# Storing x2 and its logits batch by batch: 64-row transfers in place of two-batch transfers in a delta-attention and two-MoE kernel

## The chip, the cores and the metric

The kernel runs on one core of a Trainium2 chip, as one program. The metric is device time in microseconds (us) of one execution. Before the change the median of three runs is 911.99 us (910.92 to 912.21).

## What is computed

Three stages follow one another (B = 4 batches, 8 heads, S = 768 positions, head size 48; 3072 tokens of 384 features):

```python
for t in range(S):                                    # attention: a delta rule per head
    y[:, :, t] = einsum('bhd,bhde->bhe', q_t, state)
    v_old = einsum('bhde,bhd->bhe', state, k_t)
    state += b_t * outer(k_t, v_t - v_old)
x = y.transpose(0, 2, 1, 3).reshape(B * S, 384)       # tokens: batch-major
h = x @ w_in; x2 = (h * sigmoid(h)) @ w_out           # first MoE: 384 -> 2048 -> 384
logits = x2 @ w_gate; e = argmax(logits)              # second MoE: eight experts, top 1
out = x2, and for tokens with x2 @ w_skip > 0:
out += softmax(logits)[e] * (relu(x2 @ w1[e]) @ w2[e])
```

Products are made in float32 accuracy by splitting each operand into a high and a low part (`gh`/`gl`, `exh`/`exl`, `ew`), so one product takes three matmul groups.

## The kernel before

**Stages.** The sequence is cut into 12 chunks of 64 positions (`NCH`, `CH`). In `period(c)` attention of chunk c runs beside the first MoE of chunk c-1 (`l1`, `l2`: sixteen blocks of 128 hidden features) and the finish of chunk c-2. One chunk holds 4 x 64 = 256 tokens, as columns of the tile `x`. After the last chunk `moe(NCH - 1)` and `finish(NCH - 1, ...)` run with no attention beside them; then comes the expert stage: for each of the eight experts, gather its tokens, transpose them, two products, and a scatter of the results into `out`.

**Finish of a chunk.** `x2out` (lines 718 to 739) takes the 256 columns in two halves `hf`. A half holds the 64 positions of batch 2*hf and the 64 positions of batch 2*hf + 1. TensorE transposes it and multiplies by the gate and skip weights at once (`xr`); ScalarE copies the 384 features and VectorE sums the ten logit columns into the tile `xs`, 128 partitions x 394 floats: partitions 0 to 63 are one batch, 64 to 127 the other. Two transfers then leave from SyncE: `x2s<-xs`, all 394 columns, into a table in DRAM from which the experts gather, and `out_dram<-xs`, the 384 features, into the result. `route1` and `route2` find each token's expert and its place, and `scatter` writes token numbers into the lists `lst` by an indirect transfer from GpSimd.

**After the last chunk.** `index_last` (line 772) computes the experts' token numbers `idx_t` on TensorE and VectorE, without going through `lst` for the last chunk. `warm(30)` issues 30 small matmuls. GpSimd then issues six indirect gathers `xg<-x2s,idx_t` (`gather_e`, line 894, experts 0 to 2, two halves each). A gather reads any row of `x2s`, so it can start only when every store into `x2s` has landed. `tr_e` transposes the gathered rows (`etp`), `el1` and `el2` are the two products (`ehp`, `yp`), `eout` writes the results.

**Weights of the experts.** `load_e` loads one expert's weights in eight pieces of 384 KB (`eraw`, eight buffers), ScalarE and then VectorE or GpSimd split a piece (`ew`), which frees its buffer for the next expert. For expert 1 GpSimd's splits are placed behind the gathers.

**What sets the order.** Every engine and every queue works in order. From chunk 2 on, the class `InOrder` keeps instructions as the Python code issues them; its helper at line 43 records every operation, so nearly all rows of the profile read L43 and are told apart by tile names. The rest is ordered by a scheduler; in the last two finishes it puts `out_dram<-xs` of half 0 ahead, since that needs ScalarE's copy alone. All plain transfers leave by SyncE's one queue (SPq), in order. They name a view of DRAM:

```python
ov = out.rearrange("(b s) f -> b s f", b=B)[2 * hf:2 * hf + 2, c * CH:(c + 1) * CH, :]
sv = x2s.rearrange("(b s) f -> b s f", b=B)[2 * hf:2 * hf + 2, c * CH:(c + 1) * CH, :]
nc.sync.dma_start(out=sv, in_=xs)
nc.sync.dma_start(out=ov, in_=xs[:, 0:DM])
```

Of the kernel before, what the change touches and what calls it, by code (L numbers as in the profile page):

```python
# [57 lines left out]
def kernel(  # L58
# [25 lines left out]
    nc = InOrder(tc)  # L84
    NCH, B, _, _, NP, CH = qk.shape
    D = ki.shape[-1]
    H, S = 2 * NP, NCH * CH
    NTOK, DM = out.shape
# [32 lines left out]
    x2s = dram.tile([NTOK, WX], F32, name="x2s")  # L121
# [591 lines left out]
    def x2a(c):  # L713
        xt = x2_t[c, "t"] = rot.tile([128, KD, B * CH], F32, tag="k3", name="xt")
        nc.vector.tensor_copy(out=xt[:, 0:2], in_=mm[c][0])
        act_copy(out=xt[:, 2], in_=mm[c][1][:, 0])

    def x2out(c):

        if (c, "t") not in x2_t:  # L720
            x2a(c)
        xt = x2_t.pop((c, "t"))
        for hf in range(2):
            ts = slice(hf * 128, (hf + 1) * 128)
            xp = ps_1.tile([128, KD, 128 + NL], F32, tag="l1", name="xr")
            for jj in range(KD):
                nc.tensor.matmul(xp[:, jj], lhsT=xt[:, jj, ts], rhs=iwg[:, jj], start=True, stop=True)
            xs = rot.tile([128, WX], F32, tag="k15", name="xs", bufs=2)
            seen["x2"] = nc.scalar.activation(
                out=xs[:, 0:DM].rearrange("p (j f) -> p j f", j=KD), in_=xp[:, :, 0:128], func=AF.Copy  # L730
            )
            nc.vector.tensor_reduce(
                out=xs[:, DM:WX], in_=xp[:, :, 128:].rearrange("p j e -> p e j"), axis=AX.X, op=ALU.add
            )
            ov = out.rearrange("(b s) f -> b s f", b=B)[2 * hf:2 * hf + 2, c * CH:(c + 1) * CH, :]
            sv = x2s.rearrange("(b s) f -> b s f", b=B)[2 * hf:2 * hf + 2, c * CH:(c + 1) * CH, :]
            nc.sync.dma_start(out=sv, in_=xs)
            nc.sync.dma_start(out=ov, in_=xs[:, 0:DM])
            x2_t[c, hf] = xs

    def route1(c):
# [384 lines left out]
    def finish(c, part):  # L1126
        if part == 0:
            x2out(c)
        elif part == 1:
            route1(c)  # L1130
        else:
            route2(c)
# [200 lines left out]
    for j in range(2):  # L1333
        nc.sync.dma_start(
            out=idx_h[:, j],
            in_=lst[j].rearrange("(e r) c -> e (r c)", e=NE)[:, 0:CAP].rearrange("e (p a) -> p e a", a=2),
# [6 lines left out]
    for part in range(3):  # L1343
# [7 lines left out]
        out=cnt_i, in0=ct, scalar1=float(127 - CAP), scalar2=None, op0=ALU.add  # L1351
# [111 lines left out]
```

## Time and profile before

| | |
|---|---|
| median of three runs | 911.99 us |
| the profiled execution, its own time | 911.39 us |
| its span (first to last instruction) | 909.6 us |
| TensorE matmul (PE) busy | 816.8 us, 90% of the span |
| TensorE weight load (PEld) busy | 780.5 us, 86% |
| VectorE (DVE) busy | 619.0 us, 68% |
| ScalarE (ACT) busy | 473.6 us, 52% |
| GpSimd (POOL) busy | 367.9 us, 40% |
| stores `x2s<-xs` | 24, of 197.0 KB |
| stores `out_dram<-xs` | 24, of 192.0 KB |

The busy shares are means over stages with different limits; PE and PEld overlap. KB are units of 1024 bytes. [...] A duration of an SPq row is the time that the queue's sequencer took to issue the transfer, not the time of the transfer.

### The profile page before, as it was taken

The numbers are of one execution on the slowest core, as the hardware profiler recorded it, in microseconds if no ns is written. First come the engines' busy times: TensorE is split into PE (matmuls) and PEld (weight loads), VectorE is DVE, ScalarE is ACT, GpSimd is POOL, SyncE is SP. The second block draws the span as 40 slices with busy tenths as digits, with TensorE's granted clock in tenths as the row PEclk, the third lists the DMA queues.
The fourth block names the chain that finished last, engine by engine and source line by source line (L and its number), as shares of the span: only waits on it lengthen the run. The fifth ranks groups of instructions, "written<-read, shape, count | busy, mean of one in ns | idle before, by whom it ended". The sixth has DMA issues, their size and how long they took to land. (4 is left out here: it accounts for less than half of the span.)

```text
span 909.6 us, 25993 instructions
## 1 busy us (share of the span) xinstructions
PE 816.8 (90%) x10385; PEld 780.5 (86%) x10385; DVE 619.0 (68%) x1776; ACT 473.6 (52%) x1290; POOL 367.9 (40%) x533
## 2 busy tenths in 40 slices
PE   8175978798899999999999999999999939999994
PEld 8174977797899999999999999999998938999994
DVE  4998895797777978777786877779223018765731
ACT  3257974336464655647465665745454334555520
POOL 5477663141333334333333333334336333454320
PEclk6565898898999999999999999999999968999998
DMA  8963211122230414132140414120036116766300
GB/s 296 399 212 108 77 31 34 55 58 64 80 125 18 127 53 139 51 104 90 31 145 27 132 51 139 53 65 19 29 111 204 19 51 192 257 208 218 112 21 24
DMA packets 64914, 96.09 MB, mean 106 GB/s; under 512 B 9290, under 2 KB 46232, under 8 KB 64784
## 3 DMA queue, kind: packets, MB, share of 16 engines
q1 hardware_dynamic: 61968, 89.69, 31.0%
q0 software_dynamic: 2816, 4.65, 1.7%
q8 instruction: 83, 1.36, 0.6%
q14 instruction: 47, 0.39, 0.2%
HBM read 80.79 MB, written 12.91 MB: 103 GB/s over the span
## 5 line engine op out<-in xcount | busy, mean ns | idle before, releaser
L43 POOL TENSOR_TENSOR gl<-gf,gh 128x256 fp32r<-128x256 f32 x192 | 149.7, 780 | 347.9 <-ACT gf L43 305.9
L43 PE MATMUL hp<-x,w 128*128 128x256 f32 x1728 | 256.5, 294 | 7.2 <-DMA x<-x 2.7
L43 PEld LDWEIGHTS hp<-x,w 128*128 128x128 f32 x1728 | 224.6, 194 | 15.3 <-DVE xs L43 4.4
L43 PE MATMUL xp<-gh,w 128*128 128x256 f32 x1152 | 172.1, 285 | 6.7 <-ACT gh L43 6.3
L43 PEld LDWEIGHTS xp<-gh,w 128*128 128x128 f32 x1152 | 153.6, 192 | 7.9 <-ACT gh L43 6.9
L43 DVE SCALAR_TENSOR_TENSOR tmp<-X,nw,Gi 128x126 f32<-128x126 f32 (+22 forms) x341 | 137.2, 402 | 10.4
L43 ACT ACTIVATE gh<-hp 128x256 fp32r<-128x256 f32 x192 | 73.3, 382 | 136.1 <-PE hp L43 135.2
L43 DVE TENSOR_TENSOR X<-X,tmp 128x126 f32<-128x126 f32 (+22 forms) x341 | 102.6, 301 | 8.6
L43 PE MATMUL xp<-gl,w 128*128 128x256 f32 x576 | 103.9, 288 | 2.1 <-POOL gl L43 2.0
L43 PEld LDWEIGHTS xp<-gl,w 128*128 128x128 f32 x576 | 83.2, 192 | 3.9 <-POOL gl L43 3.0
L43 ACT ACTIVATE gf<-hp 128x256 f32<-128x256 f32 x192 | 72.7, 379 | 4.7 <-POOL gl L43 4.6
L43 PE MATMUL ehp<-exh,ew 128*128 128x256 f32 x384 | 66.9, 284 | 0.0
L43 ACT ACTIVATE SU<-St 32x192 f32<-32x192 f32 (+1 forms) x176 | 63.6, 361 | 2.7
L43 ACT ACTIVATE ew<-eraw 128x768 fp32r<-128x768 f32 x64 | 53.3, 843 | 21.0 <-PE yp L43 15.4
L43 PE MATMUL g<-kq,KtB 128*128 128x128 f32 (+1 forms) x384 | 55.5, 303 | 8.9 <-DVE PQ L43 5.6
L43 DVE COPY_PREDICATED PQ<-mU,g 128x512 f32<-128x512 uint8 x44 | 32.2, 738 | 45.3 <-ACT G L43 39.1
L43 DVE TENSOR_TENSOR ew<-eraw,ew 128x768 fp32r<-128x768 f32 x48 | 49.9, 1046 | 18.0 <-ACT ew L43 12.0
L43 PEld LDWEIGHTS g<-kq,KtB 128*128 128x128 f32 x384 | 52.1, 216 | 10.1 <-DVE PQ L43 6.2
L43 DVE TENSOR_TENSOR vp<-vp,ru 64x192 f32<-64x192 f32 x92 | 31.5, 345 | 41.7 <-PE ru L43 38.5
L43 PEld LDWEIGHTS ehp<-exh,ew 128*128 128x128 f32 x384 | 58.8, 191 | 0.0
L43 PE MATMUL yp<-ew,egh 128*128 128x384 f32 x256 | 57.6, 342 | 0.3 <-ACT egh L43 0.3
L43 POOL TENSOR_TENSOR ew<-eraw,ew 128x768 fp32r<-128x768 f32 x16 | 30.2, 1892 | 57.0 <-ACT ew L43 56.7
(144 smaller groups left out, 1283.6 us busy)
## 6 DMA issues: line engine op xcount, KB each, us to landing
eraw<-in_w_dram SPq DMA_DIRECT2D x64, 384.0 KB
kq<-in_qk_dram SPq DMA_DIRECT2D x44, 256.0 KB
PQ<-in_qp_dram SPq DMA_DIRECT2D x44, 256.0 KB
ki<-in_ki_dram SPq DMA_DIRECT2D x44, 192.0 KB
raw<-in_w_out_dram SPq DMA_DIRECT2D x16, 384.0 KB
raw<-in_w_in_dram SPq DMA_DIRECT2D x16, 384.0 KB
x2s<-xs SPq DMA_DIRECT2D x24, 197.0 KB
v<-in_v_dram SPq DMA_DIRECT2D x24, 192.0 KB
```

Source lines behind the costliest of these rows:

```text
L43: r = f(*args, **kw)
```

## The change

Each of the two stores of a half becomes two stores, one per batch: 64 partitions of `xs` into 64 consecutive rows of `x2s`, or of `out`. The same bytes go to the same places.

```diff
-            ov = out.rearrange("(b s) f -> b s f", b=B)[2 * hf:2 * hf + 2, c * CH:(c + 1) * CH, :]
-            sv = x2s.rearrange("(b s) f -> b s f", b=B)[2 * hf:2 * hf + 2, c * CH:(c + 1) * CH, :]
-            nc.sync.dma_start(out=sv, in_=xs)
-            nc.sync.dma_start(out=ov, in_=xs[:, 0:DM])
+            for i in range(2):
+                t0 = (2 * hf + i) * S + c * CH
+                nc.sync.dma_start(out=x2s[t0:t0 + CH, :], in_=xs[i * CH:(i + 1) * CH])
+            for i in range(2):
+                t0 = (2 * hf + i) * S + c * CH
+                nc.sync.dma_start(out=out[t0:t0 + CH, :], in_=xs[i * CH:(i + 1) * CH, 0:DM])
```

On SyncE's queue, the finish of an early chunk (here the first one in the program), as a piece of the difference; the shapes are those of the DRAM side:

```order
 L43 DMA x<-x 16x3x512 x2
-L43 DMA x2s<-xs 2x64x394
-L43 DMA out_dram<-xs 2x64x384
-L43 DMA x2s<-xs 2x64x394
-L43 DMA out_dram<-xs 2x64x384
+L43 DMA x2s<-xs 64x394 x2
+L43 DMA out_dram<-xs 64x384 x2
+L43 DMA x2s<-xs 64x394 x2
+L43 DMA out_dram<-xs 64x384 x2
 L43 DMA kq<-in_qk_dram 128x512 x2
 L43 DMA v<-in_v_dram 128x384
```

Four issues became eight; what stands ahead and behind is the same.

On SyncE's queue, the finish of the last chunk, before:

```order
L43 DMA idx_h<-lst_86 128x8x2
L43 DMA out_dram<-xs 2x64x384
L43 DMA x2s<-xs 2x64x394 x2
L43 DMA out_dram<-xs 2x64x384
L43 DMA eraw<-in_w_dram 128x3x256
```

and with the change:

```order
L43 DMA idx_h<-lst_86 128x8x2
L43 DMA out_dram<-xs 64x384
L43 DMA x2s<-xs 64x394 x2
L43 DMA out_dram<-xs 64x384
L43 DMA x2s<-xs 64x394 x2
L43 DMA out_dram<-xs 64x384 x2
L43 DMA eraw<-in_w_dram 128x3x256
```

The last `x2s` store was third of the four and is now sixth of the eight: ahead of it stand four 64-row stores of half 0 and one of its own half. Apart from SyncE's queue, the instructions of all engines stand in the same order as before.

## Rows read from the trace of the kernel before

**Rows 1.** Busy time by stretch (us, engines' busy us and counts, PEclk, DMA share, GB/s)

```profile
250.00:300.00 50.00, 49.75 (x770) 47.50 (x769) 38.60 (x120) 29.51 (x89) 18.98 (x31) 1.00 0.25 79
727.00:750.00 23.00, 7.95 (x57) 6.94 (x56) 5.00 (x29) 8.71 (x13) 7.35 (x9) 0.67 0.15 48
800.00:850.00 50.00, 49.19 (x352) 48.67 (x350) 32.41 (x65) 28.25 (x54) 21.79 (x16) 1.00 0.67 205
```

**Rows 2.** Waits, 715 to 790 us (us in total, times, longest)

```profile
PE etp L43 <- DMA xg<-x2s,idx_t: 12.0, 3, 11.3
POOL xg L43 <- DMA x2s<-xs: 10.3, 1, 10.3
```

**Rows 3.** Timeline around the gathers (start, us, instruction, idle before and releaser)

```profile
729.31 0.52 SPq L43 DMA_DIRECT2D out_dram<-xs  x1
...
729.95 2.94 SPq L43 DMA_DIRECT2D x2s<-xs  x2
...
730.02 0.19 DVE L43 TENSOR_REDUCE xs<-xr 128x10 f32<-128x30 f32 x1
...
734.52 3.36 PE L43 MATMUL g<-one 128*128 128x128 bf16 x30
734.56 0.97 POOL L43 DMA_INDIRECT lst<-ids,si  x1 [0.30 <-issue]
734.71 0.17 DVE L43 TENSOR_TENSOR idx_t<-idx_f,px 128x16 int32<-128x16 f32 x1 [0.46 <-PE px L43]
745.84 1.04 POOL L43 DMA_INDIRECT xg<-x2s,idx_t  x1 [10.31 <-DMA x2s<-xs]
...
749.23 0.87 PE L43 MATMUL etp<-iwg,xg 128*128 128x128 f32 x3 [11.35 <-DMA xg<-x2s,idx_t]
...
753.42 3.64 POOL L43 TENSOR_TENSOR ew<-eraw,ew 128x768 fp32r<-128x768 f32 x2
...
764.96 0.85 ACT L43 ACTIVATE ew<-eraw 128x768 fp32r<-128x768 f32 x1 [2.30 <-DMA eraw<-in_w_dram]
...
766.13 0.97 PE L43 MATMUL yp<-ew,egh 128*128 128x384 f32 x4 [0.29 <-ACT egh L43]
```

**Rows 4.** Busy time by stretch: loads at the start, and around the gathers

```profile
20.00:40.00 20.00, 5.72 (x27) 5.53 (x26) 18.73 (x66) 5.59 (x16) 5.92 (x11) 0.50 1.04 400
...
738.00:741.00 3.00, 0.00 (x0) 0.00 (x0) 0.00 (x0) 0.00 (x0) 0.00 (x0) 0.94 0.14 45
...
752.00:755.50 3.50, 3.50 (x19) 3.50 (x18) 3.31 (x7) 0.88 (x2) 3.18 (x4) 0.51 0.38 103
755.50:760.00 4.50, 4.37 (x31) 4.05 (x31) 4.50 (x8) 1.25 (x4) 1.56 (x1) 1.00 0.39 99
```

**Rows 5.** DMA in the stretch 735 to 745 us

```profile
DMA packets 365, 0.46 MB, mean 46 GB/s; under 512 B 70, under 2 KB 365, under 8 KB 365
```

**Rows 6.** Timeline of one period: SyncE's queue, and ScalarE's first use of `kq`

```profile
234.24 0.56 SPq L43 DMA_DIRECT2D x2s<-xs  x1
...
235.53 3.10 SPq L43 DMA_DIRECT2D x2s<-xs  x1
238.68 3.41 SPq L43 DMA_DIRECT2D out_dram<-xs  x1
242.14 4.30 SPq L43 DMA_DIRECT2D kq<-in_qk_dram  x2
...
255.99 0.84 ACT L43 ACTIVATE KtB<-kq 64x256 f32<-64x256 f32 x2
```

**Rows 7.** Timeline: two pairs of transfers and the instruction that waits for them

```profile
143.87 1.21 SPq L43 DMA_DIRECT2D x<-x  x2
...
147.43 0.83 PE L43 MATMUL hp<-x,w 128*128 128x256 f32 x5 [0.71 <-DMA x<-x]
...
707.74 2.71 SPq L43 DMA_DIRECT2D idx_h<-lst  x2
...
714.56 0.17 DVE L43 TENSOR_TENSOR idx_f<-idx_h 128x16 f32<-128x16 int32 x1 [13.99 <-DMA idx_h<-lst]
```

## The prediction

> **What bounds the kernel now.** I looked first at busy time by stretch, since a mean over stages tells nothing here [rows 1]. In a period of the attention TensorE is busy 49.75 of 50 us, and in the expert stage 49.19 of 50. There a faster transfer can buy next to nothing. Between the two, from 727 to 750 us, it is busy 7.95 of 23 us. That hole is where stores could matter, so the waits of that stretch came next [rows 2]: GpSimd's first gather waits 10.3 us for `x2s<-xs`, and TensorE waits 11.3 us for what the gather brings. The timeline gives the chain [rows 3]. SyncE issues `out_dram<-xs` of half 0 at 729.31 and the two `x2s<-xs` from 729.95 on. The token numbers `idx_t` are ready at 734.71 + 0.17 = 734.88, GpSimd is through with its last scatter at 734.56 + 0.97 = 735.53, and then both stand still until 745.84. TensorE's transposes follow at 749.23.
>
> Why do three stores, some 600 kB (192 + 197 + 197 KB of 1024 bytes), need 729.31 to 745.84, which is 16.5 us? In the middle of that time nothing else moves but stores, and the DMA share is 0.14 at 45 GB/s [rows 4]; over ten us it is 46 GB/s [rows 5]. A share of 0.14 of sixteen engines is a little over two engines. The loads at the start show what all sixteen do: share 1.04, 400 GB/s [rows 4]. So **these stores run on two engines of sixteen**. What sets them apart from those loads, in the order of the program, is the DRAM side: a load there names 128 rows, and the stores name 2 x 64 rows, with the 2 outermost.
>
> **The change, part by part.** It takes the 2 away: each new store names 64 consecutive rows.
>
> *The last chunk, the path that sets the end.* Ahead of the gather there are now six stores: two of `out` and four of `x2s`, with the same 600 kB. Their cost has three parts, none of which the trace shows for this shape.
>
> Wire time: 600 kB at 46 GB/s is 13.0 us, the bound from above. If the stores use all sixteen engines at the same rate each, it is an eighth, 1.6 us, and most of it runs while SyncE is still issuing.
>
> Issue: six issues follow one another from 729.31 on. An `x2s` store that meets an empty queue takes 0.56 us [rows 6], and `x<-x` takes 1.21 for two [rows 7], so I take 0.6 each: the last is issued at 732.9. The logits of half 1 are summed by 730.21 [rows 3] and don't hold it up. With 0.7 each it would be 733.5.
>
> Landing: `x<-x` is issued by 145.08 and TensorE waits for it until 147.43, 2.35 us [rows 7]. `idx_h<-lst` is issued by 710.45 and used at 714.56, 4.1 us [rows 7]; but it was behind stores of the chunk before. I take 2.35, the nearer one, since it met no stores: 732.9 + 2.35 = 735.25.
>
> That lies under the 735.53 at which GpSimd ends its scatter. So **the next that is late is GpSimd**: with the 0.30 that it pauses between two such transfers [rows 3] the gather starts at 735.83, which is **10.0 us earlier** than 745.84. With the worst of both parts (733.5 + 4.1) it starts at 737.6, 8.2 us earlier.
>
> *What hangs on the gather.* TensorE comes 3.4 us behind the gather's start, so at 739.2, and `warm` ends at 734.52 + 3.36 = 737.88, ahead of it. GpSimd's splits of expert 1 stand right behind the six gathers, at 753.42, and free the weight buffers, so the loads of expert 2 move up by the same 10.0 us. From there on TensorE is the bound and the whole expert stage moves as one block.
>
> *The clock.* [...] After the change the gap is 739.2 - 737.9 = 1.3 us, and in 738 to 741 the granted clock was 0.94. If the high level lasts, the 3.50 us of full work in 752 to 755.5 take half, which would give up to 1.75 us. I count nothing for it: at 764.96 ScalarE still waits 2.30 us for weights, TensorE's `yp` waits behind it at 766.13 [rows 3], and the loads of those weights move with GpSimd, not with TensorE. The 1.75 stays as the far end.
>
> *The other eleven chunks.* Four more issues each, at 0.6 us, are 2.4 us more on SyncE's queue, and `kq` stands behind them. Now the last two stores of a chunk hold the queue for 3.10 and 3.41 us and the two `kq` for 4.30 [rows 6], because two engines are backed up; with sixteen that goes, some 8 us against 2.4. Even without that the cover is wide: `kq` is issued by 246.44, lands at about 248.8 and is first used at 255.99, 7.2 us later. If that cover were gone, each us over it would be one in every period. As TensorE has 0.25 us of idle time in 50, I count neither a gain nor a loss.
>
> **Sum.** The profiled execution took 911.39 us (span 909.6, and 1.8 around it). 911.39 - 10.0 = **901.4 us**. The median of the runs is 0.6 above this execution, so 902.0 would be as good a reading; with the late landing it is 903.2, or 903.8 against the median; with the whole of the clock 899.6.
>
> [...]
>
> **Rivals.**
> 1. *The halves spread, but not over all engines, or land late.* With four engines 600 kB take 6.5 us; the 3.5 us that the old stores took beyond their wire time (16.5 - 13.0) come on top, and the gather starts at 739.3: 904.9 us. With eight it starts at 736.1, which is the forecast again. Nothing in the trace speaks for four, but nothing shows a store of 64 rows either.
> 2. *The halves don't spread.* Were it the store's direction or its 1.5 KB rows that keep two engines busy, and not the 2 x 64, the six would be as slow as the three, and the backed-up queue would hide the extra issues: 911.4 us. Against it: the share is this low only where stores that name 2 x 64 run alone.
> 3. *Slower: the halves don't spread, and each pays for itself.* The place is the same wait for `x2s<-xs`; the price is three more transfers ahead of the gather. At 0.6 us each (issue alone) the time is 913.2, at 2.35 each (a landing that nothing overlaps) 918.5. It decides from 0.6 us each on, since three times that is 1.8 us, 0.2% of the time, about what a measurement of this kernel can tell from no change. For it speaks only that the row counts are the same on the SBUF side; against it that the queue now takes a second store while the first still runs.
>
> [...]
>
> **How the numbers follow.** Forecast 0.81, rival 1 with few engines 0.07, rival 2 0.07, rival 3 0.05. The forecast and rival 1 are faster by over 0.2%: 0.88; within 0.2%: 0.07; slower: 0.05. The range for 8 in 10 is the forecast's own, from the clock's far end to the late landing against the median: 899.4 to 904.0. Rivals 2 and 3 and most of rival 1 lie outside it.
>
> **What would show it.** In the profile after, the wait of GpSimd's `xg` for `x2s<-xs` is gone or under 2 us, and the first gather starts at 735.8 to 737.6. In the us behind 730 the DMA share passes 0.5 for a short while, and no stretch of ten us at 0.14 is left. SyncE's issues of the second pair of stores fall from 3 us to 0.6 or less. TensorE's busy time stays near 817 us, or falls by up to 2 where the clock holds. It is wrong if the share stays at 0.14, if the gather waits for something behind 738, or if the expert stage, from the first `etp` to the end, takes over 1.5 us longer than its 160.4 us now (909.6 - 749.23), so that what is saved ahead is lost behind.

## The result and the profile after

| | before | after |
|---|---|---|
| median, beside each other (6 runs each) | 912.10 us (910.92 to 913.03) | 902.89 us (902.03 to 904.34) |
| ratio | | 0.9893, 95% interval 0.9882 to 0.9905 |
| the profiled execution, its own time | 911.39 us | 903.69 us |
| its span | 909.6 us | 902.0 us |
| TensorE matmul busy | 816.8 us | 811.0 us |
| stores of `x2s` and of `out` | 24 and 24 | 48 and 48 |

The change makes the kernel 9.2 us faster here. It was measured twice more, beside the experiments, and gained 6.8 us (905.5 us against 912.3, ratio 0.9927, 0.9909 to 0.9945) and 7.0 us (904.81 against 911.78, ratio 0.9928, 0.9905 to 0.9951). So the sign is sure; the size was 6.8 to 9.2 us.

The timeline of the kernel after, around the last stores and the gathers (start in us, duration, engine, instruction, idle time before it and what ended that):

```profile
729.00 0.69 DVE L43 COPY xt<-xp 128x512 f32<-128x512 f32 x1 [16.94 <-PE xp L43]
731.27 0.47 SPq L43 DMA_DIRECT2D out_dram<-xs  x1
731.84 1.19 SPq L43 DMA_DIRECT2D x2s<-xs  x2
733.08 0.59 SPq L43 DMA_DIRECT2D out_dram<-xs  x1
733.78 1.20 SPq L43 DMA_DIRECT2D x2s<-xs  x2
735.02 1.24 SPq L43 DMA_DIRECT2D out_dram<-xs  x2
...
735.22 1.00 POOL L43 DMA_INDIRECT lst<-ids,si  x1 [3.93 <-DVE si L43]
735.85 0.17 DVE L43 TENSOR_TENSOR idx_t<-idx_f,px 128x16 int32<-128x16 f32 x1
736.52 0.98 POOL L43 DMA_INDIRECT lst<-ids,si  x1 [0.30 <-DMA x2s<-xs]
737.80 1.05 POOL L43 DMA_INDIRECT xg<-x2s,idx_t  x1 [0.30 <-issue]
...
742.23 1.51 PE L43 MATMUL etp<-iwg,xg 128*128 128x128 f32 x6 [3.59 <-DMA xg<-x2s,idx_t]
```

The same landmark in the kernel before, `xt`, VectorE's copy of the last chunk's rows ahead of the transposes:

```profile
727.03 0.69 DVE L43 COPY xt<-xp 128x512 f32<-128x512 f32 x1 [12.30 <-PE xp L43]
```

`xt` comes 2.0 us later in this profile, so what lies behind it is counted from `xt`. The first gather was at `xt` + 18.81 (745.84 in [rows 3]) and is now at 737.80 - 729.00 = `xt` + 8.80: 10.01 us closer. GpSimd's wait of 10.3 us for `x2s<-xs` [rows 2] has no counterpart any more. The gather starts 0.30 us behind the end of the last `lst` scatter (736.52 + 0.98 = 737.50), the pause that stands between two such transfers in these rows. The six stores ahead of it took six issues of about 0.6 us.

That the transfers spread shows in the DMA share (busy time by stretch of the kernel after: the stretch, its length, busy us and count for PE, PEld, DVE, ACT and POOL, TensorE's granted clock as a share of full speed, the DMA share as the mean busy share of the core's sixteen DMA engines, GB/s):

```profile
733.00:734.00 1.00, 0.30 (x2) 0.11 (x2) 0.97 (x9) 0.99 (x3) 0.00 (x0) 1.00 0.78 169
735.00:736.00 1.00, 1.00 (x15) 1.00 (x15) 0.66 (x4) 1.00 (x2) 0.78 (x1) 1.00 0.75 166
```

0.78 of sixteen engines stands where 0.14 stood [rows 4]. A share adds up the time of packets and can read above 1 (1.04 in [rows 4]), so by itself it tells two engines from many, but not eight from sixteen. The small packets of 4 bytes settle that (DMA of the kernel after, 731.00 to 736.60 us, in which six of the stores land):

```profile
DMA packets 523, 0.67 MB, mean 119 GB/s; under 512 B 96, under 2 KB 523, under 8 KB 523
```

The 96 small packets are sixteen for each of the six stores; all others are rows of 1.5 KB. The whole span fits: it has 10730 packets under 512 B in place of 9290, and sixteen for each of 96 new stores less two for each of 48 old ones is 96 x 16 - 48 x 2 = 1440, just that difference. The trace's semaphore records say the same. The first new store raises its semaphore sixteen times as its data land, from 733.13 to 733.38; the two old `x2s` stores raise theirs twice each, at 740.37 and 740.40 and at 744.81 and 744.85. Read as one landing for each engine, which the old share of 0.14 (2.2 of sixteen) fits, the old stores ran on two engines, and the new ones run on sixteen. The last of the new `x2s` stores has landed by 736.55, ahead of the scatter's end.

From 250 to 300 us, in the attention, matmuls take 49.75 of 50 us as in [rows 1]. The views of the transfers say how soon one store lands (KB each, median us from issue to landing):

```profile
x2s<-xs SPq DMA_DIRECT2D x48, 98.5 KB, 2.3
out_dram<-xs SPq DMA_DIRECT2D x48, 96.0 KB, 2.2
```

In a period of the attention the queue holds no store for 3 us any more, as it did in [rows 6]; two stores go out in 1.2 us, and `kq` behind them is issued 2.9 us earlier (timeline of one period after):

```profile
236.72 1.19 SPq L43 DMA_DIRECT2D x2s<-xs  x2
237.95 1.24 SPq L43 DMA_DIRECT2D out_dram<-xs  x2
239.24 1.85 SPq L43 DMA_DIRECT2D kq<-in_qk_dram  x2
```

**Where 10.0 us became 7.6 in the profiles.** From `xt` to the gather the new kernel wins 10.01 us. `xt` itself is 1.97 us late. From the gather to the first `etp` it takes 4.43 us where it took 3.39, a loss of 1.04. From there to the end it takes 159.8 us where it took 160.4, a gain of 0.6. 10.01 - 1.97 - 1.04 + 0.60 = 7.60, which is 909.6 - 902.0. The experiments ask which of these belong to the change.

### The profile page after: what moved, and what is told of

It reads as the page before. It is cut to its first block, busy times and chain, and to the rows that moved or that the text cites. A ratio compares the mean times of both kernels' runs of the same rounds, so it can differ in the third digit from the quotient of the medians.

```text
span 902.0 us, 26074 instructions
## 1 busy us (share of the span) xinstructions
PE 811.0 (90%) x10385; PEld 775.4 (86%) x10385; DVE 618.6 (69%) x1776; ACT 474.8 (53%) x1290; POOL 367.3 (41%) x533
## 2 busy tenths in 40 slices
DMA packets 66355, 96.10 MB, mean 107 GB/s; under 512 B 10730, under 2 KB 47672, under 8 KB 66224
```

## The experiments

The theory is that of the prediction: the outermost count on the DRAM side sets how many engines a store uses, and the last chunk alone matters. The rivals: the gain sits in the eleven earlier chunks, or smaller transfers as such are what helps. Landmarks of all profiles, in us, each from the timeline of that kernel (the last column is the time that TensorE's granted clock spent at its low level, 0.50, within 28 us behind the first `etp`, added up from stretches of 2 us; a stretch at 0.75 counts half):

| kernel | gather from `xt` | gather to `etp` | `etp` to the end | clock low |
|---|---|---|---|---|
| before | 18.81 | 3.39 | 160.4 | 6.2 |
| after | 8.80 | 4.43 | 159.8 | 4.1 |
| after, again | 8.81 | 4.06 | 165.5 | 10.3 |
| after, a third time | 8.79 | 4.28 | 163.2 | 11.4 |
| last chunk alone | 8.80 | 4.26 | 166.0 | 10.2 |
| last chunk alone, again | 8.80 | 4.26 | 163.1 | 12.4 |
| all but the last | 18.94 | 3.36 | 161.3 | 5.6 |
| 62 + 2 rows | 19.13 | 3.34 | 161.8 | 5.1 |
| 48 + 16 rows | 10.59 | 3.21 | 161.8 | 5.6 |
| `x2s` alone | 10.92 | 3.72 | 159.7 | 6.4 |
| gather first | 7.84 | 3.13 | 161.7 | 3.4 |
| 60 idle products | 8.80 | 7.73 | 162.0 | 8.4 |
| gather first, 40 products | 8.58 | 3.12 | 161.8 | 1.0 |

**1. The last chunk alone, and all but the last.** The new stores in the last chunk only, against the kernel before (shortened); for the other kernel the condition reads `c < NCH - 1`:

```diff
+            if c == NCH - 1:
+                for i in range(2):
+                    t0 = (2 * hf + i) * S + c * CH
+                    nc.sync.dma_start(out=x2s[t0:t0 + CH, :], in_=xs[i * CH:(i + 1) * CH])
...
+            else:
...
+                nc.sync.dma_start(out=sv, in_=xs)
+                nc.sync.dma_start(out=ov, in_=xs[:, 0:DM])
```

> The stores of the last chunk alone are made batch by batch; the other eleven chunks keep the transfers of two batches. Theory (two engines instead of sixteen matter only where the gather waits for the last chunk's stores): the whole gain is there, 901.5 to 904 us; the first gather starts 8.8 us behind the copy of xt as in the changed kernel, and the DMA share in the periods shows long stretches of 0.14 again. Rival A (a part of the gain comes from the other chunks, whose loads stand behind the slow stores): 905 us or more. Rival B (in the other chunks the split costs something, as the 1.4 us that the changed kernel's profile lost between 234 and 267 us might say): 901.5 us or less.

> The mirror of the run before: eleven chunks batch by batch, the last chunk as before the change. Theory: 911 to 913 us, within 0.1% of the kernel before, and GpSimd's gather waits about 10 us for x2s again. Rival A: 910 us or less. Rival B: over 913 us.

Measured beside a before of 911.93 us: the last chunk alone 906.41 us (ratio 0.9929, 0.9907 to 0.995), all but the last 912.54 (1.001, 0.9993 to 1.0027). By its time alone the first lies where rival A put it, at 905 us or more; experiment 4 takes that up. The second shows that the new stores in the eleven earlier chunks buy nothing and cost nothing that can be measured, and the gather of the first comes as early as the changed kernel's (8.80 us): the gain is the last chunk's. The place shows in the timeline of the kernel with all but the last:

```profile
730.57 2.66 SPq L43 DMA_DIRECT2D x2s<-xs  x2
746.50 1.04 POOL L43 DMA_INDIRECT xg<-x2s,idx_t  x1 [10.44 <-issue]
```

The old stores of the last chunk hold up the gather as before. (The 10.44 us are put down to "issue" here, and to the stores in [rows 2]; the gather is where it was either way.)

**2. Smaller, or divisible?** The last chunk's stores are cut once more, into 62 + 2 rows, or with 48 in place of 62 into 48 + 16; the stores of `out` are cut likewise. Both make eight stores of a half where the change makes four.

```diff
-                nc.sync.dma_start(out=x2s[t0:t0 + CH, :], in_=xs[i * CH:(i + 1) * CH])
+                for r0, r1 in ((0, 62), (62, CH)) if c == NCH - 1 else ((0, CH),):
+                    nc.sync.dma_start(out=x2s[t0 + r0:t0 + r1, :], in_=xs[i * CH + r0:i * CH + r1])
```

> Still batch by batch, but in the last chunk each store of 64 rows is cut into 62 rows and 2 rows. If the number of engines is a divisor of the outermost count up to 16, 62 rows run on two engines as 2 x 64 did: the DMA share behind 732 us is about 0.13, the gather starts 17 to 20 us behind the copy of xt (before: 18.8), and the time is 911 to 914 us. Rival (what was slow was a transfer over two batches, not its outermost count): the stores stay fast, the six more issues ahead of the gather cost at most 6 x 0.6 = 3.6 us, 903 to 907 us.

> The control for 62 and 2: the same number of transfers and bytes in the last chunk, cut into 48 rows and 16 rows, both of which divide by 16. Theory: all engines are used (share over 0.4 behind 732 us), and what is left is issue: twelve issues of 0.6 us ahead of the gather instead of six, so x2s lands about 3.6 us later than in the changed kernel, of which some 0.5 us are covered by GpSimd's scatter: 905 to 907 us. Rival (issues are hidden): 902.5 to 903.5 us. If 62 and 2 and this one take the same time, the outermost count isn't the cause.

62 + 2 rows: 912.73 us, ratio 1.0007 (0.9993 to 1.0021). 48 + 16 rows: 904.58 us, ratio 0.9913 (0.9888 to 0.9938). With the same number of transfers and the same bytes the two differ by 8 us. Timeline with 62 + 2 rows:

```profile
732.01 5.82 SPq L43 DMA_DIRECT2D x2s<-xs  x4
744.92 1.04 POOL L43 DMA_INDIRECT xg<-x2s,idx_t  x1 [10.63 <-DMA x2s<-xs]
```

and with 48 + 16:

```profile
733.76 1.77 SPq L43 DMA_DIRECT2D x2s<-xs  x4
738.34 1.05 POOL L43 DMA_INDIRECT xg<-x2s,idx_t  x1 [2.10 <-DMA out_dram<-xs]
```

and the DMA share while TensorE has nothing to do, with 62 + 2 rows:

```profile
736.00:744.00 8.00, 0.00 (x0) 0.00 (x0) 0.00 (x0) 0.12 (x1) 0.00 (x0) 0.50 0.13 47
```

So it is not the size of a transfer. 62 rows are as slow as 2 x 64, at a share of 0.13 and 47 GB/s, and 48, 16 and 64 rows are fast. The small packets tell the engines apart here too. Over the span there are 10730 under 512 B in the changed kernel, 10634 with 62 + 2 rows and 10858 with 48 + 16. With sixteen for each store of 64, 48 or 16 rows and two for each of 62 or 2 rows, the stores of the last chunk have 8 x 16 = 128, 16 x 2 = 32 and 16 x 16 = 256, and 128 - 32 = 96 and 256 - 128 = 128 are the two differences. That fits a divisor of the outermost count up to sixteen, as the expectation for 62 + 2 rows had it; no run stores with another count. The additional issues ahead of the gather cost 10.59 - 8.80 = 1.8 us, less than the 3.1 us that the expectation left uncovered: four of these smaller stores in a row took 1.77 us, 0.44 each and not 0.6.

**3. What the store of `out` costs.** Only `x2s` is stored batch by batch; `out` leaves in the old form:

```diff
-            for i in range(2):
-                t0 = (2 * hf + i) * S + c * CH
-                nc.sync.dma_start(out=out[t0:t0 + CH, :], in_=xs[i * CH:(i + 1) * CH, 0:DM])
+            ov = out.rearrange("(b s) f -> b s f", b=B)[2 * hf:2 * hf + 2, c * CH:(c + 1) * CH, :]
+            nc.sync.dma_start(out=ov, in_=xs[:, 0:DM])
```

> Only the stores of x2s are batch by batch; those of out keep two batches in a transfer. The store of out that stands ahead of them then holds two engines for 197 kB / 46 GB/s = 4.3 us, and each x2s store has a sixteenth on either of these. Theory (engines work their shares in order): x2s lands some 2 us later than in the changed kernel, the gather 9.5 to 11.5 us behind xt (8.8 in the changed kernel, 18.8 before), 903.5 to 906 us. Rival (only the x2s stores' own engine count matters): 8.8 us, 902 to 904 us.

904.22 us, ratio 0.9915 (0.9896 to 0.9934), beside the changed kernel's 905.5 in the same series. The gather is at `xt` + 10.92 and waits for stores again (timeline):

```profile
731.09 3.58 SPq L43 DMA_DIRECT2D x2s<-xs  x4
739.08 1.05 POOL L43 DMA_INDIRECT xg<-x2s,idx_t  x1 [2.42 <-DMA x2s<-xs]
```

One `out` store in the old form, ahead in the queue, holds up the `x2s` stores that follow (the four issues take 3.58 us, in place of 1.19 + 1.20), so that the gather comes 2.1 us later than in the changed kernel, and yet the end does not come later. What comes behind the gather differs by more than that from one profile to the next, as the table shows, so how much the `out` part adds to the time stays open; that it moves the gather by 2.1 us is shown.

**4. Is the stage behind the gather longer?** In the first series the last chunk alone came 3.5 us above the changed kernel's first result, with its gather at the same place. Both kernels run once more, side by side and unedited.

> The changed kernel once more, on the same chip and beside the same runs of before as the next one. The last chunk alone measured 906.4 us, 3.5 us over the changed kernel, though its gather stood at the same distance from xt (8.80 us); its expert stage, first etp to the end, took 166.0 us where the changed kernel's took 159.8. Theory A (the length of the expert stage differs from run to run and doesn't depend on how the other chunks were stored): both kernels come out within 1.5 us of each other, at 902 to 907 us. Theory B (the other chunks' stores matter once the last chunk is fast): this one stays at 902 to 904 us and the other stays 2 us or more above it.

> The last chunk alone batch by batch, once more. Theory A: within 1.5 us of the changed kernel of the same call. Theory B: 2 us or more slower, with the expert stage at 164 us or more in its profile and TensorE waiting for the gathers inside the stage (4 us in the first profile, against 1 us in the changed kernel).

905.5 us (0.9927, 0.9909 to 0.9945) and 906.45 us (0.9939, 0.9922 to 0.9955). Side by side they are 0.95 us apart, within either interval, so the earlier 3.5 us did not come back and nothing speaks for the eleven chunks. The profile of the changed kernel, taken again, loses its time right behind the gather. Its timeline:

```profile
741.71 0.55 PE L43 MATMUL etp<-iwg,xg 128*128 128x128 f32 x3 [0.19 <-DMA xg<-x2s,idx_t]
743.52 1.00 POOL L43 DMA_INDIRECT xg<-x2s,idx_t  x1 [0.30 <-issue]
744.54 3.60 POOL L43 TENSOR_TENSOR ew<-eraw,ew 128x768 fp32r<-128x768 f32 x2
744.63 0.49 ACT L43 ACTIVATE exh<-etp 128x384 fp32r<-128x384 f32 x1 [6.17 <-remote]
745.16 0.56 DVE L43 TENSOR_TENSOR exl<-etp,exh 128x384 fp32r<-128x384 f32 x1 [3.20 <-issue]
745.63 2.55 DVE L43 TENSOR_TENSOR gd<-xg,gmx 128x16 f32<-128x16 f32 x1
745.82 0.87 PE L43 MATMUL etp<-iwg,xg 128*128 128x128 f32 x3 [3.56 <-DVE exl L43]
748.10 0.55 DVE L43 TENSOR_TENSOR exl<-etp,exh 128x384 fp32r<-128x384 f32 x1
```

The transposes are done at 741.71 + 0.55 = 742.26, but ScalarE's `exh` (the high part), whose input they are, begins at 744.63. It waits for something that the trace calls "remote", and names no tile and no transfer of the program. TensorE then stands 3.56 us behind it. In the first profile of the changed kernel `exh` follows its transposes at once:

```profile
743.14 1.13 ACT L43 ACTIVATE exh<-etp 128x384 fp32r<-128x384 f32 x2 [3.81 <-PE etp L43]
744.30 0.56 DVE L43 TENSOR_TENSOR exl<-etp,exh 128x384 fp32r<-128x384 f32 x1
744.97 4.11 DVE L43 TENSOR_SCALAR gg<-gg 128x2 f32<-128x2 f32 x1
745.40 3.65 POOL L43 TENSOR_TENSOR ew<-eraw,ew 128x768 fp32r<-128x768 f32 x2
```

The last two rows show another hold, which is older than the change: VectorE's `gg` on 128 x 2 numbers takes 4.11 us and ends at 749.08, GpSimd's split at 749.05. Before, it was `gd` that ended beside the split (757.10; the split of [rows 3] at 753.42 + 3.64 = 757.06):

```profile
753.53 3.57 DVE L43 TENSOR_TENSOR gd<-xg,gmx 128x16 f32<-128x16 f32 x1
```

In eleven of the thirteen profiles a `gd` takes 1.23 to 4.12 us, where most others take 0.16 to 0.18, and in all eleven it ends 0.02 to 0.05 us behind a split of GpSimd. That it is held until the split is through is read from these ends; `gg` begins ahead of the split, during the last gather's issue, and is held as well. What ties the two engines together, no run here shows.

What the long stages have in common is where this hold falls. Each half of the first expert needs an `exl` of VectorE (the low part) before TensorE can go on. In the first profile of the changed kernel the second `exl` is through at 744.86, ahead of the split; in the profile taken again `gd` stands between the two, takes 2.55 us in place of 0.17, ends with the split, and the second `exl` begins at 748.10. Over all thirteen profiles the second `exl` begins 6.9 to 7.1 us behind the first `etp` in the four whose stage takes 163.1 us or more, and 2.1 to 3.0 us behind it in the nine others; the first `yp` follows at 11.3 to 11.6 us in the four and at 6.9 to 8.9 in the nine. In three of the four the late `exh` is what puts `gd` beside the split. In the fourth, the first profile of the last chunk alone, the first `exh` was not held up, and `gd` was held for 4.12 us (timeline):

```profile
741.58 4.12 DVE L43 TENSOR_TENSOR gd<-xg,gmx 128x16 f32<-128x16 f32 x1
742.08 3.58 POOL L43 TENSOR_TENSOR ew<-eraw,ew 128x768 fp32r<-128x768 f32 x2
745.63 0.55 DVE L43 TENSOR_TENSOR exl<-etp,exh 128x384 fp32r<-128x384 f32 x1
```

So the rows show where the long stages lose their time: ahead of the second `exl`, where VectorE stands behind GpSimd's split. That is read from the profiles; no run moved the split to test it.

**5. Is it the clock, and can more idle products hold it?** The granted clock behind the first `etp` differs as well. After, first profile (`etp` at 742.23):

```profile
744.00:746.00 2.00, 1.68 (x8) 1.71 (x9) 1.96 (x5) 0.98 (x3) 1.68 (x3) 0.50 0.40 114
746.00:750.00 4.00, 2.27 (x19) 2.06 (x18) 3.96 (x6) 0.41 (x2) 3.05 (x2) 0.95 0.46 135
```

After, again (`etp` at 741.00):

```profile
743.00:747.00 4.00, 1.18 (x5) 0.91 (x6) 1.84 (x2) 0.98 (x2) 3.67 (x4) 0.50 0.30 88
...
751.00:753.00 2.00, 2.00 (x10) 2.00 (x10) 2.00 (x5) 0.88 (x2) 0.00 (x0) 0.50 0.00 0
753.00:757.00 4.00, 4.00 (x29) 4.00 (x29) 2.43 (x9) 1.78 (x4) 0.00 (x0) 0.98 0.79 228
```

The low level lasts until 753, 12 us behind the first `etp`; in the first profile it lasts 4 us. TensorE is busy 1.18 of 4 us behind the fall, and full from 751 on, until 753 at a granted 0.50. To test it, TensorE gets more idle products ahead of `etp` in the changed kernel. A second kernel takes the gather earlier: the four `x2s` stores of a chunk stand ahead of all `out` stores but the first, and the two `lst` scatters of the last chunk behind the gathers. It ran with the old 30 products in the series of experiment 4, and with 40 here.

```diff
-    warm(30)
+    warm(60)
```

```diff
+        for hf in range(2):
+            xs = x2_t[c, hf]
             for i in range(2):
                 t0 = (2 * hf + i) * S + c * CH
                 nc.sync.dma_start(out=out[t0:t0 + CH, :], in_=xs[i * CH:(i + 1) * CH, 0:DM])
...
-        if not nc.on:
+        if not nc.on and c < NCH - 1:
...
+        if e == 0:
+            with tc.issue_after(seen["gather"].ins):
+                scatter(NCH - 1)
```

> The changed kernel, with what is late next taken out: in every finish the four x2s stores are issued ahead of the out stores of half 1 and of batch 1 of half 0, and the last chunk's two scatters into lst, which only the overflow code reads, are issued behind the gathers. Theory (behind the stores GpSimd's two scatters are the next bound): the gather starts when x2s has landed or idx_t is ready, 7.1 to 7.6 us behind xt instead of 8.8, and the time is 1 to 1.5 us under the changed kernel of the same call. Rival (the gain is eaten in the expert stage, by the second split that now stands behind the scatters, or by the out stores that run beside the gathers): no gain.

> The changed kernel a third time, as the measure for the two kernels beside it. Its two profiles so far differ by 5.7 us in the expert stage (159.8 and 165.5 us from the first etp to the end). Theory A (the stage begins at the low level of TensorE's clock, and how long that lasts differs from one execution to the next: in the stretches of 2 us behind the first etp the granted clock is back at 1.00 after about 4 us in the first profile and after about 12 in the second): 902 to 907 us by the median, and the profile's etp-to-end time lies near 160 if the clock is back within 6 us, near 165 if it takes over 10. Rival B (the stage's length has nothing to do with the clock): the two don't go together.

> The changed kernel with 60 in place of 30 of the idle products of a matrix of ones by itself that TensorE runs ahead of the transposes. At 0.10 to 0.11 us each they end near xt + 13.5 instead of xt + 10.5, so TensorE's hole of 2 to 3.6 us in front of the first etp (xt + 13 to 14) all but closes; the gather stays at xt + 8.8. Theory A (what is given back behind the gather is the low level of the clock): the granted clock in the 12 us behind the first etp is 0.85 or more on average (0.83 in the first profile of the changed kernel, 0.57 in the second), etp to end 158 to 161, and 1.5 to 5 us less than the changed kernel on this chip. Rival B (the stage hangs on ScalarE, GpSimd and the weights): within 1 us of the changed kernel, whatever the clock. Rival C (the products run on at the low level past the arrival of the rows): first etp 0.5 to 3 us later, and slower than the changed kernel by as much.

> The order of e5 (all x2 stores ahead of the logits', the last scatter behind the gathers), with 40 idle products instead of 30. Its gap in front of the first etp was 1.0 us (products end 738.12, etp 739.11), so ten more at 0.11 us just close it. Theory A: gather at xt + 7.8 as in e5, first etp at xt + 11, the clock back at 1.00 within 6 us, 899 to 902.5 us, the fastest of the three. Rival B: as e5, 2 to 3 us under the changed kernel, since the gain is the gather's alone. Rival C: the products push the first etp back by up to 1 us and it loses that against e5's lead.

The gather first: 902.54 us (0.989, 0.9871 to 0.9909), 3.0 us under the changed kernel of its series. Beside a before of 911.78: the changed kernel a third time 904.81 us (0.9928, 0.9905 to 0.9951), with 60 products 904.89 (0.9924, 0.9898 to 0.995), the gather first with 40 products 902.7 (0.9901, 0.9877 to 0.9924). So 30 more products change nothing. The gather first was 3.0 and 2.1 us under the changed kernel of its series; in the first pair no run of one reaches the other's, in the second the runs overlap, so the size is not sure. In the profiles its first `etp` comes at `xt` + 10.97 and + 11.70 where the changed kernel's comes at + 12.87 to + 13.23.

With 60 products, the timeline of TensorE shows why this does not test the clock:

```profile
732.78 5.11 PE L43 MATMUL g<-one 128*128 128x128 bf16 x52
738.88 0.38 PE L43 MATMUL g<-one 128*128 128x128 bf16 x4 [1.00 <-issue]
740.31 0.38 PE L43 MATMUL g<-one 128*128 128x128 bf16 x2 [1.05 <-issue]
...
741.82 0.42 PE L43 MATMUL etp<-iwg,xg 128*128 128x128 f32 x1
```

The last eight of the 60 come in pieces, with waits for "issue" that no data explains, and push the first `etp` to `xt` + 16.5 instead of about `xt` + 13. And the clock was low for 8.4 us behind it all the same, so this kernel did not set up what it was to test: the clock as a cause is neither shown nor refuted by it. Better evidence is the table. Where the clock was low for 1.0 to 8.4 us the stage took 159.7 to 162.0 us, in no order: 1.0 us low went with 161.8, 6.4 us low with 159.7. In the kernel with 40 products the high level lasted almost throughout, and the first `yp` came 7.33 us behind the first `etp`, where it came at 7.18 before the change with 6.2 us at the low level. So the high level alone bought nothing there. Where it was low for over 10 us, in four profiles, all of kernels with the early gather and 30 products, the stage took 163.1 to 166.0; these are the four of experiment 4 in which VectorE stood behind the split. In three of those four `exh` waited some 6 us, ended by "remote", and began about 0.1 us behind the end of the last gather's issue; in the fourth the second `exh` did so for 0.96 us. The third run of the changed kernel is one of the three: its `exh` waits 6.13 us, the clock is low for 11.4 us and the stage takes 163.2, between the two values that its expectation named.

The holds and a long spell at the low clock come together. While TensorE stands idle for `exl`, as between 743 and 747 us above, a slower clock cannot be what it waits for; how much of the rest the clock adds, and what ScalarE waits for, no run here settles.

The gather first goes as far as the chain allows. In its timeline the gather now stands behind the token numbers, and not behind a scatter:

```profile
730.98 2.48 SPq L43 DMA_DIRECT2D x2s<-xs  x4
734.99 0.17 DVE L43 TENSOR_TENSOR idx_t<-idx_f,px 128x16 int32<-128x16 f32 x1
735.98 1.06 POOL L43 DMA_INDIRECT xg<-x2s,idx_t  x1 [5.55 <-DVE idx_t L43]
```

It came 0.82 us behind them (734.99 + 0.17 = 735.16), at `xt` + 7.84, a little later than the 7.1 to 7.6 expected. With 40 products the gather came at `xt` + 8.58. The profile puts it down to a store of `out`, but again it stands 0.83 us behind the token numbers (740.92 and 741.75); these were later, since the products `px` that make them took 1.43 us at a granted clock of 0.54 (738.87 to 740.87 us) where they had taken 0.81 at 0.95. Both medians (902.54 and 902.7) are the lowest of their series, and hardly under the changed kernel's first (902.89). It is the best version found.

## Why the prediction came out as it did

It forecast 901.4 us, or 902.0 against the median of the runs, in a range of 899.4 to 904.0. The first result, 902.89, lies in it; the two later medians, 905.5 and 904.81, lie 1.5 and 0.8 us above it. So the mechanism was right, and that the time fell into the range is in part luck: the profile of the first result is the one of three in which the stage behind the gather did not get longer.

- **Two engines because of the 2 x 64: right.** The share went from 0.14 to 0.78 in single microseconds, the landings per store from two to sixteen, and 62 rows brought the old time back.
- **Wire time 1.6 us, at the old rate for each engine: not shown, and hidden.** From 733 to 734 us the stores moved 169 GB/s at a share of 0.78, which is 169 / (0.78 x 16) = 13.5 GB/s for an engine's worth of busy time; the old ones moved 46 / (0.14 x 16) = 20.5. It cost nothing, since the data moved while SyncE was still issuing and GpSimd was later still.
- **Issue 0.6 us each: right.** Six issues run from 731.27 to 734.98, 3.7 us (3.6 forecast).
- **Landing 2.35 us: right.** The median is 2.3 us.
- **GpSimd's scatter is late next: right.** The gather starts 0.30 us behind it.
- **The gather 10.0 us earlier: right,** 10.01 us counted from `xt`, and 10.00 to 10.02 in the five other profiles of kernels with the new stores in the last chunk, uncut and in the order of the change.
- **The other eleven chunks at nothing: right,** 912.54 against 911.93 us with the new stores there alone.
- **"The whole expert stage moves as one block": wrong, by 1 to 3 us of the 10 in the medians.** This is the term that was mis-sized. From the gather to the first `etp` it takes 4.1 to 4.4 us in five profiles where it took 3.4, so 0.7 to 1.0 us is given back at once. In the stage behind that, the change's own profiles take 159.8, 165.5 and 163.2 us against 160.4. The first part goes with the scatter: in all five the gather starts 0.30 us behind the last `lst` scatter, and where the scatter is 2.1 us or more ahead of it or behind the gathers, the step takes 3.1 to 3.7 us. No run changed the scatter alone, so this is read from the table and not shown by an experiment. The second part is VectorE's: the prediction let GpSimd's splits move up with the gathers and counted only the buffers that they free, not that VectorE stands beside them, for up to 4.12 us (`gd` in the first profile of the last chunk alone). Whether that hurts depends on whether the second `exl` gets in ahead of them. The prediction named this as what would make it wrong ("over 1.5 us longer than 160.4") and gave it no price.
- **The clock, a gain of 0 to 1.75 us: the bound was one-sided.** The 1.75 us is half of the 3.50 us that [rows 4] has at a granted 0.51, with 1.00 behind it, and no run shows it: where the high level lasted (the gather first with 40 products), the stage took 161.8 us. The first profile had the low level for 4.1 us in place of 6.2, the second and third for over 10. The gap ahead of `etp` was forecast at 1.3 us; it was 3.59 in the first profile, since the gathered rows came later.
- **The rivals.** Few engines and no spread are refuted by the landings, the share and the gather. The slower one, by which three more transfers ahead of the gather each pay, fails at its place: the gather does not wait for them.

Nothing puts the loss of 1.97 us ahead of `xt` in the profiles down to the change. In the thirteen profiles `xt` lies between 725.3 and 733.2 us with new stores in the earlier chunks, and between 725.7 and 728.5 with the old ones; the three of the changed kernel are at 729.00, 728.13 and 726.52. In the profile of the result one stretch of 8 us had the clock at 0.76, which is 0.24 x 8 = 1.9 us less work at full speed, and 101 products where 113 were done before:

```profile
234.00:242.00 8.00, 7.76 (x101) 7.36 (x101) 2.18 (x14) 1.96 (x6) 2.81 (x6) 0.76 0.60 136
```

The same stretch before:

```profile
234.00:242.00 8.00, 7.73 (x113) 7.33 (x114) 3.64 (x23) 2.29 (x8) 2.80 (x6) 1.00 0.12 36
```

The new stores don't always bring this on: with all but the last chunk changed, the stretch had them in it and a granted clock of 1.00.

## What to carry to other kernels

Where a DMA share stays near an eighth while a transfer is waited for, look at the outermost count on the DRAM side: here a leading 2 held a transfer of 128 partitions at a share of 0.14, two engines of sixteen, and cutting it along that 2 cost 0.6 us of issue for each more store and brought the gather 10 us closer here. It pays only where somebody waits, here at one chunk in twelve. When a long wait is taken away, look right behind it, where 1 to 3 us came back here: first at what stood second in line, here a scatter, and then at what now falls together, here GpSimd's splits and VectorE's small instructions.

## What the runs showed that was not expected

- Identical kernels differ behind the gather: 5.7 us between two profiles of the changed kernel from `etp` to the end, with the gather at `xt` + 8.80 and 8.81.
- ScalarE's `exh` waited up to 2.4 us beyond its input (742.26 to 744.63), ended by nothing of the program, and TensorE's independent products came in pieces from 737.9 us on, while gathers were in flight (60 products). What either waited for is open.
- A shorter store is issued faster: 0.44 us each for 48 and 16 rows (1.77 for four), 0.62 for 64 (2.48 for four, with the gather first), where the queue isn't backed up.
